# Seven products in place of eight for a second pair of batches, in part of the columns, in a polysketch attention and wave MLP kernel

## The chip, the cores and the metric

One core of a Trainium2 chip runs the whole program. The metric is device time in microseconds, the median of several runs; less is better. The engines work side by side, each through its own list of instructions in order: TensorE (PE; its weight loads are PEld), VectorE (DVE), ScalarE (ACT), GpSimd (POOL) and SyncE (SP, which here only starts transfers).

## What is computed

Four batches of 1088 tokens. An attention with polynomial sketches gives x (128 features a token); x then goes through a mixing step over the tokens. All weights come as float64, and the result is held to float32 accuracy.

```python
def phi(x):                                   # 8 x 8 = 64 features of a head's 32
    a, b = einsum('rd,bhsd->bhsr', S1, x), einsum('rd,bhsd->bhsr', S2, x)
    return einsum('bhsi,bhsj->bhsij', a, b).reshape(..., 64)
kv, z = einsum('bhsf,bhsd->bhfd', phi(k), v), phi(k).sum(2)
x = (phi(q) @ kv) / (phi(q) . z + 1e-06)      # (4, 1088, 4 * 32)
theta = x @ w_theta
y = w_tok_r @ (x * cos(theta)) + w_tok_i @ (x * sin(theta))   # both 1088 x 1088
u = x + y
out = u + relu(u @ w_ch)
```

The costly part is y: for each batch a product of the real and the imaginary token weights, 2 x 1088 x 1088, with z, which is x turned by cos and sin.

## The kernel before

**Lists, not loops.** The program records every operation with its engine and its operands (`Layout.op`), and then issues them in an order written out by hand as numbers (`ORDER`), with the buffer of each temporary given in `PLACES`. Nothing is scheduled at run time: an engine takes its instructions in this order and waits where an operand is not ready or a buffer not free. Nearly all instructions carry the line of a small helper: 312 (matrix product), 292 (VectorE, two tensors), 296 (VectorE, tensor and scalars), 299 (VectorE, `scalar_tensor_tensor`, two tensors and a scalar), 306 (a transfer by POOL that adds to its target). So groups are told apart by their tiles.

**Stages.** For each batch k, q and v are loaded, k is summed into features (`kfeatures`, `key_sums`, `chain`), q is turned and split (`query_slices`), multiplied (`levels`, with the denominator), and `outputs_x` gives x transposed (tile xT, features on partitions, 1152 columns) and from it theta, cos and sin and z. z has 17 chunks of 128 tokens by 128 features: 8 real, 8 imaginary and one of remainders (64 tokens of each). The token weights come as 17 rows w0 to w16 of 128 x 1088, real 0 to 7, imaginary 8 to 15 and 16 the remainders. A row arrives as float64 in a raw buffer (class zs, five in all, which the z of the batches share), ScalarE reads it twice (lines 555 and 557), and VectorE puts it together as float32 (a shift at line 296 and a custom operation at 292).

**Mixing.** For batches 0 and 1, `mix_row` multiplies chunk i of z with row i for all 17 rows into PSUM, in spans of 384, 384 and 320 columns: batch 0 takes all three spans at one row (three PSUM banks), batch 1 a span at a time. These products need only a finished row and the batch's z, and so they fill PE's list while VectorE and ScalarE prepare later batches. `mix_out` adds y to x: for both batches ScalarE copies y out, and POOL adds x by a transfer (`UDMA`). `finish` multiplies with w_ch, applies relu, transposes on VectorE and stores by four transfers from SP.

**The pair 2, 3.** These two batches take one step of Winograd's form of Strassen's scheme. The weights are seen as four quarters: a11 and a12 are the real and imaginary rows in output columns 0 to 543, a21 and a22 in 544 to 1087. With z of batch p (2) and q (3) as the other matrix, seven products of 8 chunks replace eight. They need sums of quarters (`asum`, 8 operations of 544 columns on VectorE each, written over a21 and a12) and differences of z (`zsub`, three operations each). Every product is made in two column parts (`PARTS`: 288 and 256 columns). Products 1 and 2 need neither sums nor differences; 5 needs the first of both, 6 the second, 3, 7 and 4 the later ones. `add` adds each result to xT. So that the differences lose no accuracy, q's z is scaled by a power of two that brings it to p's size: `balance` takes the largest magnitude of x of each batch by two reductions on VectorE, makes the ratio, ScalarE scales x before the turn, and `add` takes the factor out again.

Of the kernel before, what the change touches and what calls it, by code (L numbers as in the profile page):

```python
# [9 lines left out]
F32 = mybir.dt.float32  # L10
# [19 lines left out]
    "6 4 2 5 44 0 1 47 342 3 45 7 50 8 347 49 9 10 11 58 12 29 48 13 76 83 14 46 70 64 15 84 86 16 133 87 77 85 71 "  # L30
    "26 17 139 146 30 89 88 19 72 140 78 73 343 147 74 90 21 18 149 134 27 345 79 91 94 25 150 20 40 80 92 65 32 93 "
    "31 344 41 95 99 127 148 100 43 66 157 151 337 135 22 102 158 101 67 96 128 303 42 68 103 97 348 311 35 28 104 "
    "313 105 36 304 159 305 106 315 160 350 136 108 307 161 306 107 137 109 308 59 23 129 110 314 309 24 111 316 "
    "237 61 112 312 195 33 113 98 130 231 37 238 114 225 115 131 232 152 244 34 69 116 310 233 60 239 226 75 117 "
    "196 123 118 38 81 349 119 120 122 121 346 422 234 357 240 82 424 338 351 53 352 426 425 317 423 153 340 427 "
    "339 428 154 39 429 382 62 124 155 430 141 208 156 125 431 245 201 162 432 126 189 202 197 163 190 433 165 164 "
    "198 318 358 166 191 227 63 434 209 142 359 167 203 435 132 168 436 138 228 367 204 192 169 56 437 171 170 372 "
    "354 438 172 362 143 439 441 173 452 442 174 144 440 353 175 443 51 210 176 445 453 145 444 455 178 446 177 246 "
    "456 179 448 360 447 459 449 180 341 460 461 450 454 181 462 457 182 186 463 183 185 187 184 451 361 521 464 "
    "465 519 355 522 458 466 523 520 356 467 524 468 469 484 525 369 526 527 368 485 470 528 471 377 473 188 57 529 "  # L40
    "472 486 364 530 474 220 531 487 532 363 533 221 374 534 488 392 535 373 542 538 536 549 539 543 537 545 211 "
    "544 550 212 552 546 540 553 247 551 222 215 547 541 213 365 554 548 214 248 475 555 366 556 251 572 558 477 "
    "557 559 574 489 370 560 478 561 575 479 371 564 562 480 476 216 566 563 54 481 252 567 217 249 568 199 569 581 "
    "250 378 483 604 482 605 576 375 570 565 582 218 571 577 606 379 376 573 607 578 387 583 384 579 584 580 253 "
    "393 193 235 223 194 254 224 219 394 255 261 200 265 383 262 608 397 266 205 609 268 267 264 380 585 263 610 "
    "385 206 395 269 323 207 270 389 396 611 586 324 271 321 381 319 587 320 273 588 388 272 274 241 627 322 628 "
    "275 407 390 276 490 412 229 398 831 629 386 277 589 278 399 400 279 630 631 401 402 408 590 612 280 281 632 "
    "297 391 491 835 414 832 492 409 283 410 282 413 411 417 493 403 284 415 291 404 405 494 325 406 495 292 416 "
    "419 496 285 326 286 418 833 327 287 288 290 497 420 293 421 498 289 296 52 834 294 499 500 654 501 507 652 655 "
    "508 650 653 502 298 651 633 256 656 328 634 657 513 332 299 591 658 514 635 659 257 592 660 330 661 636 662 "  # L50
    "593 258 594 55 663 259 331 595 664 333 637 665 596 666 597 673 503 598 329 638 674 334 676 669 335 667 504 639 "
    "677 336 295 505 675 230 300 236 599 668 242 670 680 678 260 243 671 679 681 672 640 688 613 687 683 641 689 "
    "684 695 690 614 691 693 714 692 682 712 694 715 697 716 713 698 301 717 685 699 718 600 686 719 515 720 703 "
    "601 696 705 721 642 700 789 302 701 706 790 516 707 704 702 791 709 780 708 722 615 781 723 616 724 711 808 "
    "517 792 710 518 809 725 617 618 726 619 506 727 810 742 643 620 735 743 728 745 782 744 793 746 838 644 736 "
    "749 621 783 737 738 622 731 729 784 645 730 747 732 739 733 740 734 811 741 798 748 799 750 800 762 751 753 "
    "764 801 765 755 785 752 756 794 766 757 623 768 754 624 758 771 836 812 773 802 759 774 813 770 760 803 761 "
    "795 775 828 763 776 772 767 848 839 777 769 840 841 837 849 778 804 829 850 860 786 851 779 842 886 843 862 "
    "787 852 857 926 830 625 646 788 853 861 796 854 858 868 855 844 856 845 859 864 814 869 797 805 863 877 865 "
    "846 647 878 889 879 870 927 871 887 904 847 880 890 881 930 872 866 806 602 894 867 882 603 883 888 873 928 "  # L60
    "874 967 815 626 807 875 932 905 884 934 509 876 895 892 818 648 896 931 906 933 907 939 929 897 937 940 891 "
    "816 885 941 510 908 935 948 909 936 949 893 898 950 938 924 819 942 910 911 943 951 899 912 952 913 944 925 "
    "953 817 945 820 954 822 821 946 900 649 947 901 968 902 955 903 970 956 957 511 980 958 512 823 971 824 981 "
    "825 982 972 983 826 919 984 920 973 969 974 959 990 961 991 975 921 976 922 923 914 992 960 915 977 916 978 "
    "917 962 979 985 964 963 827 1000 986 918 1001 987 993 965 994 988 1002 966 995 989 996 1004 997 1003 998 1005 "
    "1006 999 1007 1010 1008 1011 1012 1009 1013 1014 "
)
PLACES = (
    "3 1 9 1 1 11 1 21 2 13 15 7 1 9 1 16 6 19 4 0 5 6 0 3 6 3 4 4 1 1 11 3 2 5 6 8 2 1 0 2 4 6 5 2 2 0 7 8 0 1 7 3 "
    "5 5 2 9 6 1 0 4 6 5 7 4 2 1 12 1 7 4 2 0 0 2 0 1 8 4 4 4 3 19 2 5 4 6 14 0 6 0 5 1 7 4 11 1 2 7 8 0 0 7 1 7 21 "  # L70
    "4 0 3 3 7 5 6 1 2 2 6 3 10 12 3 2 2 3 5 8 14 3 4 4 1 4 1 2 2 0 0 6 3 2 2 9 10 5 0 4 0 0 5 21 7 10 7 6 11 3 6 1 "
    "3 0 7 7 11 1 6 4 7 2 6 7 9 5 1 0 4 4 6 7 2 3 7 0 0 2 6 5 3 0 2 3 2 0 12 2 6 8 3 11 10 0 7 18 3 17 5 1 20 17 3 "
    "16 0 4 9 11 3 2 13 2 9 15 3 19 20 1 4 1 1 9 16 1 9 2 3 9 19 2 4 4 3 9 0 7 1 2 11 4 6 0 0 3 5 3 6 0 4 3 4 4 2 2 "
    "5 2 5 6 7 3 3 1 2 7 0 3 6 5 4 3 3 0 2 2 3 5 3 1 0 4 3 2 5 9 7 4 0 4 7 0 2 2 1 2 1 1 3 0 0 7 7 1 3 2 7 2 0 7 7 "
    "4 1 4 1 3 2 3 5 0 0 5 0 1 0 6 3 7 14 6 6 0 3 1 6 5 3 4 3 1 7 1 0 2 4 7 6 1 3 0 6 5 4 5 4 2 0 6 3 4 21 1 21 1 4 "
    "2 5 2 6 2 3 6 4 4 1 1 6 5 0 4 4 3 1 0 0 4 0 6 6 0 1 7 1 4 5 7 14 2 3 0 4 6 2 5 0 2 3 2 6 4 5 4 2 1 6 3 3 2 4 7 "
    "1 5 "
)
SPINS = (
    "76:2 139:4 158:1 109:1 422:1 "  # L80
# [7 lines left out]
PAIR = (2, 3)  # L88
PARTS = ((0, 288), (288, 544))
LAST = (416,)  # L90
APOOL = ()
# [5 lines left out]
UDMA = (True, True, False, False)  # L97
# [128 lines left out]
def kernel(  # L226
# [636 lines left out]
    even = fixed((6,), F32, "even")  # L863
# [122 lines left out]
    def outputs_x(b, lv, pool_qp):  # L986
# [38 lines left out]
        src = xt  # L1025
        if b == PAIR[1]:
            src = balance()
        for g in range(NG):
# [4 lines left out]
            if src is not xt:  # L1033
                xs = buf("g1", (GW,), F32, "xs")
                op("A", act(GW), lambda g=g, xs=xs: A.mul(xs(), xt()[:, g * GW:(g + 1) * GW], even()[:, 4:5]), [xs],
                   cells(xt, g * GW, (g + 1) * GW) + [even])
                off, dep = 0, [xs]
            else:
                xs, off, dep = xt, g * GW, cells(xt, g * GW, (g + 1) * GW)

            def turn(x=x, xs=xs, off=off):
                for i in range(GC):
                    T.transpose(x()[:, i], xs()[:, off + i * P:off + (i + 1) * P], ident())  # L1043

            def theta(g=g, th=th):
# [4 lines left out]
            op("P", 0.67, theta, [th], cells(xt, g * GW, (g + 1) * GW) + [w2])  # L1050
# [11 lines left out]
            vop(2 * full * P, lambda c0=c0, full=full, cs=cs, x=x: tt(  # L1062
                V, z()[:, 0:2 * NF].rearrange("p (t c) d -> p t c d", t=2)[:, :, c0:c0 + full],
                bc(x()[:, 0:full], 1, [P, 2, full, P]), cs()[:, :, 0:full], ALU.mult), [(z, (0, g)), (z, (1, g))],
                [x, cs])
            if full < GC:
                def tail(cs=cs, x=x, full=full):
                    tt(V, z()[0:TL, NK - 1], x()[0:TL, full], cs()[0:TL, 0, full], ALU.mult)
                    tt(V, z()[TL:P, NK - 1], x()[0:TL, full], cs()[0:TL, 1, full], ALU.mult)

                op("V", 0.6, tail, [(z, NG)], [x, cs])

    def balance():
        at("even")
        for j, b in enumerate(PAIR):
            vop(NC * P, lambda j=j, b=b: V.tensor_reduce(out=even()[:, j:j + 1], in_=xT[b](), axis=AX.X, op=ALU.max,
                                                         apply_absolute_value=True), [(even, j)], [xT[b]])

        def ratio():
# [278 lines left out]
```

## Time and profile before

| | us |
|---|---|
| median of 3 runs | 223.38 |
| lowest, highest | 221.67, 223.63 |
| the profiled execution, its own time | 221.87 |
| its span, first to last instruction | 220.1 |

| engine | what it does most | count | busy us | mean ns |
|---|---|---|---|---|
| PE | products of z and w, 384 / 320 / 288 / 256 columns (two records each) | 136 / 68 / 88 / 70 | 50.0 / 23.6 / 26.4 / 19.5 | 489 / 435 / 406 / 381 |
| DVE | rows of w: custom operation, shift | 17, 17 | 21.7, 12.1 | 1284, 718 |
| DVE | sums of w, 544 columns | 32 | 22.3 | 714, 710 |
| DVE | largest magnitudes (line 1076) | 2 | 2.7 | 1348 |
| ACT | rows of w, two reads | 34 | 41.3 | 1216, 1221 |
| ACT | squares with a sum (line 892), and its read | 4, 4 | 4.8, 0.9 | 1194, 226 |
| ACT | scaling of x for batch 3 (line 1035) | 3 | 1.7 | 605 |
| POOL | adding transfers, issue | 12 | 11.5 | 985, 1040 |

Busy time is counted once where records of an engine overlap. On PE records overlap by design, so their mean is longer than the distance between them.

### The profile page before, as it was taken

The numbers are of one execution on the slowest core, as the hardware profiler recorded it, in microseconds if no ns is written. First come the engines' busy times: TensorE is split into PE (matmuls) and PEld (weight loads), VectorE is DVE, ScalarE is ACT, GpSimd is POOL, SyncE is SP. The second block draws the span as 40 slices with busy tenths as digits, with TensorE's granted clock in tenths as the row PEclk, the third lists the DMA queues.
The fourth block names the chain that finished last, engine by engine and source line by source line (L and its number), as shares of the span: only waits on it lengthen the run. The fifth ranks groups of instructions, "written<-read, shape, count | busy, mean of one in ns | idle before, by whom it ended". The sixth has DMA issues, their size and how long they took to land.

```text
span 220.1 us, 5075 instructions
## 1 busy us (share of the span) xinstructions
PE 211.9 (96%) x2045; PEld 160.0 (73%) x2045; DVE 173.8 (79%) x395; ACT 116.8 (53%) x228; POOL 22.7 (10%) x44
## 2 busy tenths in 40 slices
PE   7999996999999999999999999999999999999993
PEld 3787895776678576766667668777688888788872
DVE  4799999999989998988906852899268899955651
ACT  3899989779978986646424455623484000000000
POOL 2465000000050110000222040000200000000000
PEclk9999999999999999999999999999999999999999
DMA  5999189993969763785345342003400002102453
GB/s 177 421 416 390 35 368 356 337 414 102 357 207 255 211 251 133 283 324 206 79 139 91 119 107 42 1 13 56 66 0 0 3 0 47 25 0 43 66 91 75
DMA packets 23195, 34.68 MB, mean 158 GB/s; under 512 B 17028, under 2 KB 18308, under 8 KB 20996
## 3 DMA queue, kind: packets, MB, share of 16 engines
q1 hardware_dynamic: 17908, 29.28, 37.8%
q0 software_dynamic: 1728, 4.65, 9.9%
q10 hardware_dynamic: 3536, 0.43, 1.3%
q8 instruction: 16, 0.26, 0.5%
q14 instruction: 7, 0.06, 0.1%
HBM read 27.48 MB, written 2.23 MB: 135 GB/s over the span
## 4 chain that ended last, share of the span: by engine, by line
PE 83%; DVE 11%; ACT 2%; issue 2%; POOL 1%; POOLq 0%
PE ps L312 74%; PE ps L1010 3%; DVE big L292 3%; DVE g L292 2%; PE ps L1043 2%; PE ps L350 2%; DVE lv L292 1%; PE ps L918 1%; DVE sm L299 1%; DVE hf L296 1%; DVE sm L292 1%; PE ps L694 1%; ACT big L605 1%; ACT g L697 1%; DVE big L296 0%
## 5 line engine op out<-in xcount | busy, mean ns | idle before, releaser
L312 PE MATMUL ps<-big,zs 128*128 128x384 f32 (+4 forms) x398 | 111.6, 423 | 0.4 <-DVE big L292 0.4
L312 PEld LDWEIGHTS ps<-big,zs 128*128 128x128 f32 x398 | 71.2, 190 | 26.7 <-issue 0.8
L1142 ACT COPY g<-ps 128x128 f32<-128x128 f32 (+1 forms) x3 | 0.9, 301 | 48.1 <-PE ps L1134 44.6
L557 ACT ACTIVATE big<-zs 128x1088 int32<-128x1088 uint32 (+1 forms) x18 | 21.1, 1178 | 6.4 <-DMA zs<-w_tok 4.7
L292 DVE CUSTOM_DVE_ANT_0 big<-big,big 128x2176 uint16<-128x2176 uint16 x17 | 21.7, 1284 | 1.5 <-ACT big L557 1.5
L312 PE MATMUL ps<-big,big 128*64 128x64 f32 (+2 forms) x208 | 21.6, 276 | 0.0
L555 ACT ACTIVATE big<-zs 128x1088 f32<-128x1088 f32 x17 | 20.6, 1216 | 0.2 <-DMA zs<-w_tok 0.2
L312 PEld LDWEIGHTS ps<-big,big 128*64 128x64 f32 (+1 forms) x208 | 16.7, 154 | 3.0 <-issue 0.5
L292 DVE TENSOR_TENSOR big<-big,big 128x544 f32<-128x544 f32 x24 | 16.7, 714 | 0.1
L1014 ACT COPY g<-ps 128x384 f32<-128x384 f32 x24 | 10.3, 485 | 11.1 <-PE ps L1010 10.1
L292 DVE TENSOR_TENSOR zs<-ps,g 128x768 f32<-128x768 f32 (+2 forms) x20 | 12.5, 629 | 3.0 <-ACT g L1056 2.6
L306 POOL DMA_DIRECT2D big<-hf x6 | 5.9, 985 | 82.6 <-DVE sm L296 40.7
L296 DVE TENSOR_SCALAR big<-big 128x1088 int32<-128x1088 int32 x17 | 12.1, 718 | 0.1
L292 DVE TENSOR_TENSOR g<-lv 128x768 f32<-128x768 f32 x12 | 11.0, 953 | 0.6 <-PE ps L312 0.5
L312 PEld LDWEIGHTS ps<-w,big 128*128 128x128 f32 x80 | 10.3, 192 | 1.6 <-issue 0.6
L299 DVE SCALAR_TENSOR_TENSOR g<-g,ps 128x384 f32<-128x384 f32 x12 | 6.5, 549 | 5.9 <-ACT g L1052 5.7
L312 PE MATMUL ps<-w,big 128*128 128x128 f32 x80 | 11.1, 277 | 0.0
L1052 ACT ACTIVATE g<-ps 128x384 f32<-128x384 f32 x12 | 5.7, 490 | 7.9 <-PE ps L312 5.3
L1010 PEld LDWEIGHTS ps<-ident,g 128*128 128x128 f32 x72 | 8.2, 141 | 2.3 <-issue 0.8
L1010 PE MATMUL ps<-ident,g 128*128 128x128 f32 x72 | 9.5, 275 | 0.0
L299 DVE SCALAR_TENSOR_TENSOR big<-ps,even,big 128x256 f32<-128x256 f32 (+1 forms) x10 | 4.8, 495 | 5.7 <-PE ps L312 5.7
L312 PE MATMUL ps<-g,sm 128*64 128x384 f32 x48 | 9.1, 499 | 0.0
(185 smaller groups left out, 335.6 us busy)
## 6 DMA issues: line engine op xcount, KB each, us to landing
zs<-w_tok SPq DMA_DIRECT2D x17, 1088.0 KB, 7.0
big<-k_l SPq DMA_DIRECT2D x6, 576.0 KB, 5.9
big<-hf POOLq DMA_DIRECT2D x6, 576.0 KB, 5.6
big<-q_l SPq DMA_DIRECT2D x4, 576.0 KB, 8.7
big<-v_l SPq DMA_DIRECT2D x4, 576.0 KB, 11.0
g<-big POOLq DMA_DIRECT2D x4, 192.0 KB, 3.7
out<-g SPq DMA_DIRECT2D x16, 48.0 KB, 1.8
g<-big POOLq DMA_DIRECT2D x2, 160.0 KB, 3.2
```

The lines of the kernel that those rows point to most:

```text
L292: eng.tensor_tensor(out=o, in0=a, in1=b, op=f)
L296: (eng or V).tensor_scalar(out=o, in0=a, scalar1=s1, scalar2=s2, op0=op0, **kw)
L299: (eng or V).scalar_tensor_tensor(out=o, in0=a, scalar=s, in1=b, op0=op0, op1=op1)
L306: op("G", 0.9, lambda: G.dma_start(dst(), src(), accum_op=ALU.add), w, r, fly=fly)
L312: T.matmul(o, lhs, rhs, start=start, stop=stop, skip_group_check=True)
L350: T.matmul(nowhere(), idle()[:, 0:P], idle(), start=True, stop=True, skip_group_check=True)
L555: op("A", 0.22 + n * 0.0009, lambda: A.activation(dfn(), words_of(raw(), n)[1].bitcast(F32), AF.Prelu, scale=2.0**-112, alpha=-(2.0**32)), ...
L557: op("A", 0.22 + n * 0.0009, lambda: A.activation(stp(), words_of(raw(), n)[0].bitcast(U32), AF.Copy, scale=2.0**-29), [stp], [raw])
L1010: T.transpose(tr()[:, i * P:(i + 1) * P], qp()[:, i * H + 2 * n:i * H + 2 * n + 2].rearrange("p h i j -> p (h i j)"), ident())
L1014: op("A", act(GW), lambda n=n, tr=tr, qT=qT: A.copy(qT()[:, n], tr()), [(qT, n)], [tr])
L1043: T.transpose(x()[:, i], xs()[:, off + i * P:off + (i + 1) * P], ident())
L1052: op("A", act(GW), lambda cs=cs, th=th: A.activation(cs()[:, 0], th(), AF.Copy, bias=ROUND), [(cs, 0)], [th])
```

## The change

Batches 0 and 1 become a second pair (`PAIRS`). In the second column part (256 of each 544 columns, `FEW = 1`), their products are those of the seven-product scheme as well; in the first part (288 of each half) they stay direct, now in spans of 288. Since the sums of w are written over the quarters, both pairs take each step before the next sum: `winograds` goes through the steps, and at each first makes the sum and then the products of pair 0, 1 and of pair 2, 3. The differences of z for the first pair go to one buffer of class zs, for the second pair partly to smaller buffers (`spare`). For the pair 0, 1, product 5 is added to both quarters of batch 1 by VectorE, and product 3 has a bank of its own, where the pair 2, 3 goes on adding in PSUM.

The scales now come from the sum of magnitudes of all of x: ScalarE makes it for each batch with its accumulator (`AF.Abs`, the elements go to the still unused z), a product with ones adds over the partitions, and VectorE makes the ratio, once for each pair. The factor is no longer applied by ScalarE to x; the multiply that makes z takes it as a scalar operand (`scalar_tensor_tensor` in place of `tensor_tensor`) for batches 1 and 3. Batch 1's direct part takes it out on VectorE in `mix_out`, and POOL's adding transfers remain for batch 0 alone (two, of 288 columns). `ORDER`, `PLACES` and `SPINS` (idle products that keep PE running early on) are new throughout.

```diff
-PAIR = (2, 3)
+PAIRS = ((0, 1), (2, 3))
+FEW = 1
-UDMA = (True, True, False, False)
+UDMA = (True, False, False, False)
...
+        op("A", act(NC * P) + 0.12, lambda: A.activation(z()...[:, 0:NC * P], xt(), AF.Abs,
+                                                         accum_out=even()[:, b % 2:b % 2 + 1]), [z, (even, b % 2)], [xt])
+        if b % 2:
+            balance(PAIRS[b // 2], even)
+        def times(dst, x, c):
+            if b % 2:
+                stt(dst, x, even()[0:x.shape[0], 4:5], c, ALU.mult, ALU.mult)
+            else:
+                tt(V, dst, x, c, ALU.mult)
...
-                op("A", act(GW), lambda g=g, xs=xs: A.mul(xs(), xt()[...], even()[:, 4:5]), [xs], ...)
...
-            vop(NC * P, lambda j=j, b=b: V.tensor_reduce(out=even()[:, j:j + 1], in_=xT[b](), axis=AX.X, op=ALU.max,
-                                                         apply_absolute_value=True), [(even, j)], [xT[b]])
+        op("P", 0.1, lambda: mm(tot(), ones(), even()[:, 0:2], True, True), [tot], [even])
...
+        def one():
+            product("5", by, t1, a21, [(q, 1)] if p else [(q, 1), (q, 0)])
+            zsub("2", t2, im_q, t1)
...
+            product("3", by if p else each("pw"), im_q, a12, [(q, 0)], (q, 0), fresh=not p)
...
+    def winograds():
+        both = [winograd(PAIRS[0], (FEW,), (), lambda: two_in("zs")),
+                winograd(PAIRS[1], range(len(PARTS)), LAST, lambda: (spare("t1", ...), spare("t2", ...)))]
+        sums = [("1", a21, a21, a22, ALU.add), ("2", a21, a21, a11, ALU.subtract), ("4", a12, a12, a21, ALU.subtract),
+                ("3", a21, a22, a21, ALU.subtract)]
+        for k, s_ in enumerate([None] + sums):
+            if s_:
+                asum(*s_)
+            for steps in both:
+                steps[k]()
...
-        cuts = tuple(range(0, S, GW))
+        if b < 2:
+            spans = [(h * len(PARTS) + j, h * HT + c0, h * HT + c1) for h in range(2)
+                     for j, (c0, c1) in enumerate(PARTS) if j != FEW]
```

## The prediction

> **What bounds the kernel now.** First the page's shares, its 40 slices and the windows of 10 us.
>
> ```profile
> PE 211.9 (96%) x2045; PEld 160.0 (73%) x2045; DVE 173.8 (79%) x395; ACT 116.8 (53%) x228; POOL 22.7 (10%) x44
> ...
> DVE  4799999999989998988906852899268899955651
> ...
> PEclk9999999999999999999999999999999999999999
> ```
>
> ```profile
> 50.00:60.00 10.00, 10.00 (x40) 6.51 (x39) 9.68 (x18) 9.67 (x12) 0.00 (x0) 1.00 0.61 216
> ...
> 100.00:110.00 10.00, 10.00 (x34) 6.27 (x33) 9.90 (x23) 5.17 (x5) 1.30 (x1) 1.00 0.49 153
> 110.00:120.00 10.00, 10.00 (x124) 7.28 (x122) 2.79 (x7) 4.10 (x8) 2.60 (x3) 1.00 0.49 117
> ```
>
> After the size of a window stand PE's, PEld's, DVE's, ACT's and POOL's busy time. From 40 us on PE is never short of work, at full clock. But up to 110 us VectorE is full too; only then has it gaps. So there are two regimes: before 110 us both engines are full, after it PE alone. Next the timeline, VectorE's and then PE's, where these meet:
>
> ```profile
> 34.17 1.35 DVE L292 TENSOR_TENSOR big<-big,hf 128x1152 f32<-128x1152 f32 x1
> 35.44 0.45 DVE L967 TENSOR_REDUCE sm<-lv 128x36 f32<-128x288 f32 x1
> ...
> 107.93 1.29 DVE L292 CUSTOM_DVE_ANT_0 big<-big,big 128x2176 uint16<-128x2176 uint16 x1
> ```
>
> ```profile
> 92.43 21.43 PE L312 MATMUL ps<-big,zs 128*128 128x320 f32 x70
> 113.79 0.57 PE L312 MATMUL ps<-mv,hf 128*64 128x96 f16 x18
> ...
> 216.15 0.39 PE L312 MATMUL ps<-w,big 128*128 128x128 f32 x2
> ```
>
> The operation at 107.93 finishes row 16, the last row of w, at 109.2. PE multiplies it just ahead of 113.79, at about 111.95 (its 1088 columns take 1.84). So PE was 2.7 us behind VectorE there: it had other products to do, and VectorE's rows were no limit. Two prices follow. The 70 records are 35 products, 30 of batch 0 (10 rows of 1088 columns) and 5 of batch 1, 12,608 columns in 21.36 us: 1.69 ns a column. On VectorE an operation of n elements lasts n/960 + 0.15 us, and the next starts 0.085 before its end (34.17 + 1.35 against 35.44).
>
> **PE's work.** Batches 0 and 1 now cost 2 x 17 x 1088 = 36,992 columns. After: 17 rows x 576 columns x 2 = 19,584, seven products of 8 x 256 = 14,336, and four remainder rows of 256 = 1,024: 34,944. That is 2,048 columns, 3.5 us less. Two products with ones (the row of such has 248 ns) and 26 more, narrower products take back about 0.5. PE's list is **3.0 us shorter**.
>
> **Where the removed columns stood.** I added up PE's list in program order, for both kernels, up to the first product that reads row 16. Everything but w products is the same there: 55.5 us. Of w products 44.8 us stand ahead of that point before, and 31.4 after: the direct products need only a row and z, and 47% of their columns are gone; of the seven products that replace them, five wait for sums of w or of z, which come after the last row in VectorE's list. So 13.4 us of cover moves behind the point. Behind it stood 103.3 us by price, and it took 216.54 - 111.95 = 104.6. After, 10.3 more stand there (13.4 less the 3.0): **114.9**.
>
> **VectorE's list up to row 16.** It was busy 99.9 of the first 109.2 us (the windows' sums) and idle 9.4: 5.5 before 60 us, mostly at the start, and 3.9 from there on, waiting for ScalarE, rows and PE. What the change moves behind the point is four sums of w (0.714 long, 0.63 back to back): -2.5. What it puts ahead of it is nearly nothing: one scale (five tiny operations, 0.85), against fewer of the small steps of the chain, and a scalar pointer in five multiplies. That operation is not in the trace with such operands; the nearest rows are 511 ns with pointer against 456 without (288 elements), so 0 to 0.06 each; I take 0.05, 0.25 in all. Left: 97.6. The 5.5 idle stay. Of the 3.9, waits on PE vanish (PE's products that VectorE needs stand 8 us and more earlier in the lists than their use, where they stood 1.3 apart before), those on rows can stay: 0 to 3.9, and I take 0.6, since ScalarE's list up to the last row grows too. So row 16 is ready at **103.7**, 5.5 us earlier than now, while PE's list alone would be there 13.4 earlier. PE now passes the point at 111.95 with 100.3 us of work done, 11.7 of waits; then at 103.7 with 86.9, 16.8 of waits: some **5 us new**, against 3.0 of work saved.
>
> **Added on ScalarE.** Four sums of magnitudes with accumulation, by the row of the squares 1.19 + 0.23 = 1.4 each, 5.7; three scalings of 605 ns and four copies (1.8 + 2.0) go: +1.9. Two of the four stand ahead of row 16, between copies for PE. ScalarE idles 0.3 to 1.8 a window there, so I put them at nothing; without that cover it is 1.4 each on rows and copies alike, 2.8.
>
> **VectorE later.** Two reductions go (1.348 each). It gains twelve differences of z (0.55, 0.55, 0.42 four times: 6.1), nine additions of 256 columns (three at 0.408, six at 0.478: 4.1), two finishes of batch 1 (1.0), some 0.7 in the other finishes and the second scale: +10 us by these rows, on 73 busy of 110 us behind the point. It fits, but VectorE takes its list in order, and each of the four sums of w (8 x 0.63 = 5.1) must now wait until both pairs have read the old quarter; PE's next product waits behind it. Those places had slack before and after by the lists, of 0.1 to 0.5 us at six of them after. 0 to 2.4; I take 0.
>
> **Queues.** POOL loses four of its twelve additions in flight (about 1 us of issue each, 3.2 to 3.7 to land). SP issues 32 stores for batches 0 and 1 in place of 24, 0.5 each, and one group of four now stands just ahead of the two that end the program. They need 2.0 us and are ready some 2.5 earlier; 0 to 0.5, taken at 0. The end after PE's last product stays 3.6 (220.1 - 216.54).
>
> **The sum.** 103.7 + 114.9 + 3.6 = **222.2 of span**, against 220.1: +2.1, 1.0%. (From VectorE's end to PE's start it is under 0.1: the chain of waits has 215.65 + 0.30 and then 215.99.) Before, by the same sum, 109.2 + 104.6 + 3.6 = 217.4, under the 220.1 that PE's list set: this chain had 2.7 us of slack and now has none. The profiled execution took 221.87, 1.8 over its span and 0.7% under the median of 223.38, so I scale the median: 223.38 x 222.2/220.1 = **225.5**. With the ends of the unknown costs (0 and 3.9 of waits, -0.25 for the pointer; late sums and stores are rival 3): 221.4 to 225.5 of span, 224.7 to 228.9.
>
> [...]
>
> **Rivals.**
> 1. The gain arrives. Row 16 must be ready by 98.6 for the whole of it (220.1 - 3.0 = 217.1 of span, 220.3). For: the first loads are reordered, and some of the 5.5 us of early idle may go. Against: 97.6 of VectorE work leaves 1.0 for all of its waits. Row 16 at 101 would make 219.5, 222.8, no change.
> 2. Slower by more: the rows come late. A row took 5.05 and 5.2 us from issue to ScalarE's read (issues at 88.15 and 99.53, reads at 93.20 and 104.74), and three buffers carry them while five are shared with z. The last may be issued once row 12 has been read. If that is later than 95.0, then 5.2 + 2.3 + 1.2 sets row 16 and not VectorE. Were all rows as late as now, less the 2.5 of moved sums: 106.7, span 225.2, time 228.6. For: ScalarE waited 4.7 us for rows. Against: transfer engines are half idle then.
> 3. The late sums cost: PE waits 0.4 at each of six tight places, 2.4 more: span 224.6, time 227.9; with the stores' 0.5, 228.4. For: VectorE's order is fixed and now serves two pairs. Against: it idles a third of that stage.
> [...]
>
> That the change does not do what it says I rule out: the lists show seven products and the four sums.
>
> **Numbers.** Forecast 0.50; rival 1: 0.16, 2: 0.17, 3: 0.14, 4: 0.03. About 1% (221.1 to 225.6 here) is what this kernel's runs can tell from no change: they lie between 221.67 and 223.63. The forecast stands on the upper bound, so half of it, 0.25, is within 1%, and of rival 1 the partial cases, 0.05: same 0.30. Faster is the rest of rival 1, 0.11; slower 0.25 + 0.17 + 0.14 + 0.03 = 0.59. The range takes in the forecast's bounds and rivals 2 to 4 as priced; it leaves out the faster part of rival 1, 0.11, and the worst of 2, 0.05: 221.2 to 228.9.
>
> **What would show it.** Right: PE's busy share falls, with some 5 us of new waits on VectorE between 35 and 105 us; row 16 finished near 103.7; some 115 us of full PE behind it. Wrong: row 16 ready before 100, or PE waiting below 1 us a window there (rival 1); the last row's read waiting for its transfer (2); PE waiting between 140 and 200 us (3); a granted clock below 1.00 (4).

## The result, and the profile after

| | before | after |
|---|---|---|
| time, median of 20 runs each (us) | 222.32 (221.23 to 223.63) | 224.54 (223.06 to 226.59) |
| ratio, 95% interval | | 1.0103 (1.0081 to 1.0124) |
| profiled execution: time, span (us) | 221.87, 220.1 | 225.0, 223.2 |
| its mean granted clock of PE | 1.000 | 0.977 |

Slower by 1.0%; the forecast was 0.95% (225.5 on 223.38) and 222.2 us of span. On the median that the forecast started from, the ratio makes 225.7. The profiled execution is not the usual one of the changed kernel: of its 20 runs two have a clock of 0.975 to 0.977, one has 1.000 (224.06 us, 222.1 of span), and the others have 0.985 to 0.992. The page of the changed kernel, its shares and two rows of the 40 slices:

```profile
PE 214.3 (96%) x2101; PEld 173.2 (78%) x2101; DVE 180.4 (81%) x425; ACT 118.1 (53%) x229; POOL 21.6 (10%) x40
...
DVE  4898999978999999999999679726999957434642
...
PEclk9988999589999999999999999999999999999999
```

VectorE is now busy 90% or more from the 11th slice to the 22nd (56 to 123 us), and the clock is no longer full: it falls twice. PE's busy share is 96% as before, and its busy time has even risen by 2.4 us though its list is shorter, for 10.2 us of it passed at half clock (last section). In after_light, an experiment below without half clock, it is 213.0, idle products of 1.1 included. The windows that answer to those of before, and one more:

```profile
40.00:50.00 10.00, 10.00 (x124) 7.93 (x126) 8.53 (x20) 7.60 (x16) 0.00 (x0) 0.70 0.79 321
50.00:60.00 10.00, 9.63 (x90) 7.46 (x85) 8.75 (x25) 9.77 (x20) 0.00 (x0) 1.00 0.36 103
...
100.00:110.00 10.00, 10.00 (x125) 8.03 (x124) 9.86 (x25) 5.69 (x9) 0.86 (x1) 1.00 0.52 134
110.00:120.00 10.00, 10.00 (x64) 8.22 (x65) 9.50 (x26) 1.91 (x7) 1.15 (x2) 1.00 0.27 75
```

The timeline, VectorE's last row of w and then PE's places around it:

```profile
102.78 1.29 DVE L296 CUSTOM_DVE_ANT_0 big<-big,big 128x2176 uint16<-128x2176 uint16 x1
```

```profile
54.29 1.13 PE L316 MATMUL ps<-big,zs 128*128 128x256 f32 x4 [0.25 <-DVE zs L296]
...
96.47 8.89 PE L316 MATMUL ps<-big,zs 128*128 128x256 f32 x36
...
219.60 0.39 PE L316 MATMUL ps<-w,big 128*128 128x128 f32 x2
```

Row 16 is finished at 104.07 (forecast 103.7). Its first product is the last pair but one of the 36 records and starts at 104.21, 0.1 later (before: 2.7 later). From there to PE's last product it takes 115.8 (forecast 114.9), from there to the end 3.2 (forecast 3.6).

So the sum came out. But PE did not wait for row 16 itself. What last held it ahead of that row was a step of the chain, a product with ones that takes a reduction from VectorE:

```profile
95.95 0.22 DVE L808 TENSOR_REDUCE sm<-ps 128x8 f32<-128x64 f32 x1
```

```profile
96.23 0.39 PE L316 MATMUL ps<-sm,ones 128*128 128x8 f32 x2
```

From that product PE takes 7.98 us to the first pair of row 16, by price with 0.1 us of pauses in all. It takes as long in the profiles of all nine variants of the changed kernel below as well, and the pair starts 0.14 or 0.15 us after row 16 is ready, be that at 101.0 or at 105.9. So VectorE does set PE's date there, but at this step, 8 us ahead of the row that the prediction named.

Nor did the waits come where they were put. Here are the windows of the stretch from PE's first product for z to row 16, before (50.3 to 111.9) and after (54.3 to 104.2):

```profile
50.30:111.90 61.60, 61.48 (x446) 41.15 (x445) 55.67 (x109) 44.36 (x68) 5.76 (x6) 1.00 0.67 220
```

```profile
54.30:104.20 49.90, 48.99 (x430) 38.30 (x431) 49.31 (x93) 42.56 (x66) 7.08 (x6) 1.00 0.76 251
```

After the change both engines are full there: PE idles 0.9 us, VectorE 0.6. Before, VectorE had 5.9 us to spare.

To see where PE loses time I went through its operations one by one: the distance from one's start to the next one's, less the price of its kind (the 20th percentile of that distance over all operations of the kind in fourteen profiles). Besides the two kernels the table has two experiments from below, each the same kernel with idle products inside PE's waits; their clocks are 1.000 and 0.999, so they are the cleaner pair. PE's first operation starts at 1.3 us; the first two rows and these 1.3 make the third.

| us | before | after | before_light | after_light |
|---|---|---|---|---|
| list up to the first product for z, by price | 40.9 | 40.5 | 42.2 | 41.6 |
| above price up to there | 8.0 | 12.5 | 6.3 | 9.0 |
| PE's first product for z starts | 50.3 | 54.3 | 49.9 | 52.0 |
| list from there to the end, by price | 161.4 | 158.1 | 161.4 | 158.1 |
| above price, each 0.03 to 0.2 (number) | 3.4 (38) | 4.8 (54) | 3.4 (38) | 4.9 (55) |
| above price, each over 0.2 (number) | 1.0 (3) | 2.2 (5) | 1.0 (3) | 3.6 (6) |

PE's list became 3.7 us shorter, as meant (0.4 and 3.3). What ate it: 4.5 us more lost ahead of the first product for z, 1.4 in hand-offs (places where PE starts about 0.1 us later than back to back, after another engine's work), and 1.2 in new waits; PE's last product starts 3.45 us later, and the shorter end leaves 3.1 of span.

### The profile page after: what moved, and what is told of

The parts are those of the page before. It is cut to its first block, busy times and chain, and to the rows that moved or that the text cites. A ratio compares the mean times of both kernels' runs of the same rounds, so it can differ in the third digit from the quotient of the medians.

```text
span 223.2 us, 5223 instructions
## 1 busy us (share of the span) xinstructions
PE 214.3 (96%) x2101; PEld 173.2 (78%) x2101; DVE 180.4 (81%) x425; ACT 118.1 (53%) x229; POOL 21.6 (10%) x40
## 3 DMA queue, kind: packets, MB, share of 16 engines
q0 software_dynamic: 1152, 3.83, 7.3%
## 4 chain that ended last, share of the span: by engine, by line
PE 82%; DVE 7%; DMA 5%; ACT 3%; issue 1%; POOL 0%; SPq 0%; DVEq 0%
PE ps L316 72%; PE ps L1014 5%; DMA big<-hf 3%; PE ps L922 3%; DMA big<-k_l 2%; DVE big L296 1%; PE ps L1053 1%; DVE lv L296 1%; ACT big L609 1%; ACT big L896 1%; DVE g L296 1%; ACT g L701 1%; DVE big L303 1%; PE ps L698 1%; POOL big L310 0%
## 5 line engine op out<-in xcount | busy, mean ns | idle before, releaser
L316 PE MATMUL ps<-big,zs 128*128 128x288 f32 (+2 forms) x450 | 110.0, 388 | 0.6 <-DVE big L296 0.4
L316 PEld LDWEIGHTS ps<-big,zs 128*128 128x128 f32 x450 | 80.1, 190 | 18.0 <-issue 1.5
L303 DVE SCALAR_TENSOR_TENSOR big<-ps,even,big 128x256 f32<-128x256 f32 (+1 forms) x16 | 7.5, 482 | 17.0 <-PE ps L316 17.0
L316 PE MATMUL ps<-big,big 128*64 128x64 f32 (+2 forms) x176 | 13.9, 255 | 1.0 <-DMA big<-hf 0.7
L310 POOL DMA_DIRECT2D big<-hf x6 | 6.5, 1089 | 71.0 <-ACT g L1018 40.9
L1014 PEld LDWEIGHTS ps<-ident,g 128*128 128x128 f32 x72 | 9.5, 159 | 4.5 <-ACT big L714 1.7
L1014 PE MATMUL ps<-ident,g 128*128 128x128 f32 x72 | 11.6, 307 | 1.2 <-DVE sm L300 1.1
L316 PEld LDWEIGHTS ps<-big,big 128*64 128x64 f32 (+1 forms) x176 | 10.7, 147 | 2.6 <-issue 0.9
L316 PEld LDWEIGHTS <-hf 128*64 128x64 f16 (+1 forms) x288 | 8.0, 113 | 1.4 <-issue 0.9
L296 DVE TENSOR_TENSOR zs<-ps,g 128x768 f32<-128x768 f32 (+2 forms) x10 | 6.3, 630 | 3.1 <-ACT g L1066 2.9
L316 PE MATMUL ps<-big,g 128*128 128x288 f32 (+1 forms) x32 | 8.6, 396 | 0.0
```

Source lines behind the costliest of these rows:

```text
L296: eng.tensor_tensor(out=o, in0=a, in1=b, op=f)
L303: (eng or V).scalar_tensor_tensor(out=o, in0=a, scalar=s, in1=b, op0=op0, op1=op1)
L310: op("G", 0.9, lambda: G.dma_start(dst(), src(), accum_op=ALU.add), w, r, fly=fly)
L316: T.matmul(o, lhs, rhs, start=start, stop=stop, skip_group_check=True)
L1014: T.transpose(tr()[:, i * P:(i + 1) * P], qp()[:, i * H + 2 * n:i * H + 2 * n + 2].rearrange("p h i j -> p (h i j)"), ident())
```

## The experiments

All ratios are to the kernel before, measured beside each; 1.0103 is the changed kernel's own.

**Is it VectorE's list up to row 16, or PE and its clock?** Four more shifts on VectorE, in the changed kernel and in the one before:

```diff
         def shift():
             ts(dfn().bitcast(I32), dfn().bitcast(I32), 3, ALU.logical_shift_left)
+            if stage in ("row6", "row7", "row8", "row9"):
+                ts(dfn().bitcast(I32), dfn().bitcast(I32), 0, ALU.logical_shift_left)
```

> The changed kernel with the shift of rows 6 to 9 of w followed by a shift by zero bits on VectorE: four more operations of 1088 elements, 0.63 us back to back, 2.5 us ahead of row 16, the output unchanged. Theory A (VectorE's list up to row 16 sets the end): row 16 at 106.5 instead of 104.05, 2.5 us on the time, a ratio of 1.021 to 1.022 to the kernel before. Theory B (PE's own pace sets the end: the stretches in which its clock is halved, 3.3 us near 16 and 6.6 us from 39.5, and its longer list behind): VectorE has room, 0 to 0.5 us, a ratio of 1.010 to 1.013.

Measured: 226.66 us, 1.0205 (1.0157 to 1.0254): 2.1 us more. Row 16 at 105.87, 1.8 later (2.6 later if counted from the first z, which in this execution came 0.8 earlier), and PE follows 0.15 after it. PE's longest wait is for row 5 of w:

```profile
70.61 0.70 PE L317 MATMUL ps<-big,zs 128*128 128x256 f32 x2 [1.68 <-DVE big L297]
```

VectorE has no room in the changed kernel: A upwards.

> The kernel before with the same four shifts by zero bits, 2.5 us more of VectorE ahead of row 16. By the prediction its PE came to row 16 2.7 us after VectorE had it, so VectorE has room for them: A gives a ratio of 1.000 to 1.003. If VectorE's list set the end of the kernel before as well, 2.5 us and 1.011.

Measured: 224.37, 1.0102 (1.0051 to 1.0153), against the 0 that I expected. In its profile the span is 1.3 us longer: PE waits 0.61, 0.36 and 0.35 us at 73.3, 75.5 and 93.4, for z and for a step of the chain (the product with ones that is named above), though it still comes to row 16 3.4 us after VectorE (113.11 against 109.76). A part of the 1.0% is the clock. The three runs at 0.996 or more have a median of 223.14, those of the kernel before at such a clock 221.64; the three others (0.989 to 0.992) have 225.22 against 223.42. That leaves 1.5 to 1.8 us for the 2.5 that were added. So of the 2.7 us at the last row at most 1 was slack of the chain: it is tight at places ahead of it.

Then the other way, eight shifts fewer:

```diff
         def shift():
-            ts(dfn().bitcast(I32), dfn().bitcast(I32), 3, ALU.logical_shift_left)
+            if stage not in tuple(f"row{i}" for i in range(3, 11)):
+                ts(dfn().bitcast(I32), dfn().bitcast(I32), 3, ALU.logical_shift_left)
```

> The changed kernel without the shift of rows 3 to 10 of w (their products are of other numbers): eight operations of 0.63, 5.0 us of VectorE ahead of row 16. A: row 16 at 99.0, and the span falls by 5.0 from 223.2 to 218.2, as long as PE's own list (217.1 by the prediction) allows it: a ratio of 0.985 to 0.992 to the kernel before. B: no more than 0.5 us, a ratio of 1.008 to 1.010.

Measured: 223.99, 1.0073 (1.0040 to 1.0107). Row 16 is ready only 2.4 earlier, since VectorE now waits itself, longest for a product and ScalarE's copy of it:

```profile
67.84 1.48 DVE L304 SCALAR_TENSOR_TENSOR g<-g,ps 128x384 f32<-128x384 f32 x3 [2.06 <-ACT g L1068]
...
100.38 1.29 DVE L297 CUSTOM_DVE_ANT_0 big<-big,big 128x2176 uint16<-128x2176 uint16 x1
```

Of the 2.4 us, 1.0 is lost again behind row 16, where PE waits 0.7 for an addition of POOL at 107.87. A falls in this direction: 5 us less of VectorE are worth 0.3%.

**The clock.** Idle products are put ahead of an operation into its own PSUM bank, which its real product then overwrites:

```diff
+MORE = "158:1 139:1 307:1 132:3 174:3 441:6"   # operation: idle products ahead of it
...
+                    if b.cls == "ps":
+                        for _ in range(more.pop(o.i, 0)):
+                            fill(raw)
```

> The changed kernel with 15 more idle products of 384 columns on PE, ahead of six operations near 14 us and between 34 and 40 us, twelve of them ahead of PE's three longest waits there (0.51, 0.42, 1.09 us); each is 0.16 us at full clock, 2.4 in all, some 1.4 of it inside waits. They are to keep the clock from being halved near 16 and from 39.5 to 46.1 us. A, strictly: clock 1.00, but VectorE's date for row 16 stays at 104, and the time too: a ratio of 1.009 to 1.012. B: PE gains 1.6 and 3.3 us, VectorE's waits of 1.15 and 1.26 near 46 and 50 us go, row 16 is ready at 101.7, and the span is some 221: a ratio of 1.000 to 1.003.

Measured: 225.11, 1.0131 (1.0090 to 1.0171), at clocks of 0.996 to 1.000. Half clock was not what made it slower. But here 2.4 us of idle products were added (15 of 0.16: in the trace of before one takes 0.33 us at 32.59, two take 0.49 at 7.80), not all inside waits. So later only seven, inside two waits (`MORE = "174:2 441:5"`):

> The changed kernel with seven idle products, two inside PE's wait of 0.42 us at 38.0 and five inside the wait of 1.09 us at 38.8: nothing is put in where PE has work. If they keep the clock from being halved from 39.5 on, and that half clock is what the first z waits for: first w product at 51 instead of 54.3 us, time 222 to 223. If VectorE and the additions in flight take its place, as with 15 such products: 224 to 225, at a clock of 0.99 to 1.00.

Measured: 224.37, 1.0090 (1.0056 to 1.0125), clock 0.996 to 0.999. The first product for z comes 2.3 us earlier than in the changed kernel's profile, and yet the median is only 0.2 us lower. The timeline of PE, with the idle products first, and the chain of waits around 70 us:

```profile
39.02 0.97 PE L360 MATMUL ps<-idle 128*128 128x384 bf16 x5 [0.24 <-ACT sm L739]
...
51.96 1.13 PE L322 MATMUL ps<-big,zs 128*128 128x256 f32 x4 [0.25 <-DVE zs L302]
...
73.18 1.27 PE L322 MATMUL ps<-big,big 128*64 128x64 f32 x36 [1.24 <-DMA big<-hf]
...
108.42 0.72 PE L322 MATMUL ps<-g,w 128*128 128x288 f32 x2 [0.68 <-DMA g<-big]
```

```profile
64.56 1.09 POOL big L316
65.64 0.21 issue
65.86 7.18 DMA big<-hf
73.04 0.14 issue
73.18 4.75 PE ps L322 x62
```

An adding transfer that POOL issued at 64.56 takes 7.18 us (median of its kind on the page: 5.2), and PE waits for it. Against the changed kernel's profile 0.6 of the 2.3 us go again at 73.18 and 0.8 at 108.42; the span is 0.9 shorter. With PE earlier here, it is POOL's additions that it waits for (1.24 and 0.68). The same handful in the kernel before (`MORE = "166:3 172:5"`):

> The kernel before with eight idle products, three inside PE's wait of 0.66 us at 33.7 and five inside the one of 1.05 us at 37.3. Of its 41 runs 27 had a clock of 0.998 to 1.000 and 219.3 to 220.5 us of span, 12 one of 0.991 to 0.992 and mostly 221.2 to 221.8. If the idle products keep the clock up: all runs near 221.5, a ratio of 0.994 to 0.999. If they only add to PE's list: 222 to 223 and 1.000 to 1.006.

Measured: 221.40, 0.9950 (0.9923 to 0.9976), all twelve runs between 221.03 and 222.16, clock 0.997 to 1.000. **This version beats both kernels.** What it gains is the clock: the 41 runs of the kernel before at 0.997 or more have a median of 221.59 as well. The five idle products stand where PE waited 1.05 us:

```profile
37.72 0.99 PE L356 MATMUL ps<-idle 128*128 128x384 bf16 x5
```

**Is PE's list worth anything ahead of row 16?** Six of eight terms of one product are left out, once of a product at 54.8 to 87.8 us and once of one at 185 to 194 us (`THIN` names the product's stage):

```diff
-                            mm(ps()[:, o:o + w], ...)
+                            if stage != THIN or i in (0, NF - 1):
+                                mm(ps()[:, o:o + w], ...)
```

> The changed kernel without six of the eight terms of one of the seven products (rows 1 to 6 of batch 0's first product in the second column part, which stand between 54.8 and 87.8 us): 6 x 0.44 = 2.6 us less of PE ahead of row 16. Theory A (up to row 16 PE is paced by others, VectorE first, so that its own list is worth nothing there): 0 to -0.5 us, 224.0 to 224.5. Theory B (PE's list and its clock set the end from the start): -2.6, 221.9.

> The same six terms left out of a product that stands at 185 to 194 us, behind row 16: 2.6 us less of PE where it has no waits in the profile. A and B alike: -2.6 us, 221.9. If VectorE, which also finishes the output there, sets the end: less than 1 us.

Measured: ahead 224.12, 1.0097 (1.0062 to 1.0131), next to nothing; behind 223.26, 1.0026 (0.9989 to 1.0063), 0.8% less, where 2.6 us would be 1.2%. In the profile of the second (220.37, the fastest of its runs) the stretch from row 16 to PE's last product is 113.4 against 115.8, 2.4 shorter: behind row 16 PE's list counts nearly in full. In the profile of the first, waits of PE take the place of the products: among them 0.67 and 0.42 for operands from VectorE at 59.4 and 61.8, 0.42 and 0.83 for POOL's additions at 71.7 and 74.1. The same on the kernel before, with row 1 and a third of row 2 left out for batch 0 (`b, i, t0` are batch, row and first column):

```diff
             for (g, t0, t1), yp in zip(gs, yps):
+                if (b, i, t0) in ((0, 1, 0), (0, 1, 384), (0, 1, 768), (0, 2, 0)):
+                    continue
                 mm(yp()[:, :t1 - t0], z()[:, i], rows[i]()[:, t0:t1], i == 0, i == NK - 1)
```

> The kernel before without the product of row 1 for batch 0 and the first third of row 2 (1472 columns, 2.5 us of PE at 50 to 55 us). By the prediction PE came to row 16 2.7 us after VectorE: the 2.5 us arrive, 219.4 to 219.8, a ratio of 0.989. Theory D's counterpart (VectorE already paced the kernel before at places ahead of row 16, as the 2.4 us that four more shifts cost there suggest): 0 to -0.8, a ratio of 0.996 to 1.000.

Measured: 221.85 in the nine runs at a clock of 0.985 or more (222.47 in all twelve), 0.9989 (0.9954 to 1.0025). The five at 1.000 have 221.08, the kernel before at full clock 221.59: 0.5 of the 2.5 us arrive. PE comes to row 3's product early and waits there for the next part of z:

```profile
49.44 3.18 PE L313 MATMUL ps<-big,zs 128*128 128x384 f32 x10
54.55 2.10 PE L313 MATMUL ps<-big,zs 128*128 128x384 f32 x6 [1.93 <-DVE zs L293]
```

So the kernel before was not bound by PE's list alone from 40 us on, as the prediction had it. PE was hardly ever idle, but it had less than half a microsecond in hand at that z, which PE uses at 55.74 there and VectorE has ready at 55.3:

```profile
54.35 0.96 DVE L292 TENSOR_TENSOR zs<-ps,g 128x768 f32<-128x768 f32 x1
```

**ScalarE's sums.** Each sum of magnitudes over 64 of 1152 columns, alone and with the eight shifts left out:

```diff
-        A.activation(z().rearrange("p c d -> p (c d)")[:, 0:NC * P], xt(), AF.Abs, ...)
+        A.activation(z().rearrange("p c d -> p (c d)")[:, 0:64], xt()[:, 0:64], AF.Abs, ...)
```

> The changed kernel with each sum of magnitudes on ScalarE made over the first 64 of 1152 columns only: four operations of 1.22 us become some 0.35, and the first of each pair no longer waits for all three groups of columns of its batch before z may be written. The prediction put these sums at nothing: by it 0 to -0.3 us. Theory C (the sum stands on the path to the first z of batch 0, which VectorE had at 48.5 us before and at 54.2 now): the first z is ready 1 to 1.5 us earlier, and the time falls by 1 to 1.5, to 223.0 to 223.5.

> Both reliefs at once: the short sums on ScalarE, and no shift of rows 3 to 10 of w on VectorE (5.0 us). The latter alone gave 223.99. If VectorE and ScalarE together are what PE waits for, the gain now arrives: 221 to 222. If neither is, it stays at 223.5 to 224: then PE's list, its clock, or the additions in flight that POOL issues hold the rest.

Measured: 224.43, 1.0089 (1.0048 to 1.0131), and 223.42, 1.0078 (1.0051 to 1.0105). The sums are worth nothing that can be measured, as the prediction put them; theory C falls. And VectorE and ScalarE relieved by 5 and 3.5 us together still leave it slower than before.

**VectorE and PE relieved together** (the edits of after_minus and after_ahead in one kernel):

> The changed kernel without the shift of rows 3 to 10 (VectorE 5.0 us less) and without the six terms of batch 0's first product (PE 2.6 us less ahead of row 16). Alone they gave 223.99 and 224.12 against 224.54, 0.55 and 0.4. Theory D (from the first z on PE and VectorE are both full and equally long, so that either alone is worth little): together 2 to 2.6 us, 222.0 to 222.5. If neither holds the kernel there (something earlier or the additions in flight do), no more than the sum of the two: 223.5 to 224.

Measured: 223.21, 1.0045 (1.0015 to 1.0075), 0.6% less than the changed kernel, some 1.3 us: more than either alone, less than D asked for. Not settled by it.

**What all of these have in common** is the first product for z. In every profile of the changed kernel and its variants (z ready between 51.2 and 54.2) it starts within 0.1 us of the end of VectorE's operation that makes the first part of z, after a wait of about 0.25 or more. From the end of that operation to row 16 it takes 49.8 us in the changed kernel and 49.1 to 51.3 in its variants, also with eight shifts fewer, six of them behind that z (49.4), or with six terms fewer (50.0); only the four added shifts make it 52.4. So the date of row 16 follows that of the first z. Before, that z was ready at 48.5 and PE came to it at 50.3, without a wait:

```profile
50.26 5.97 PE L312 MATMUL ps<-big,zs 128*128 128x384 f32 x19
```

VectorE's timeline from the step ahead of it (44.74 before, 46.79 after) to that z (47.58, 53.29), first before, then after:

```profile
44.74 0.54 DVE L299 SCALAR_TENSOR_TENSOR g<-g,ps 128x384 f32<-128x384 f32 x1
...
45.75 1.28 DVE L292 CUSTOM_DVE_ANT_0 big<-big,big 128x2176 uint16<-128x2176 uint16 x1
46.95 0.72 DVE L296 TENSOR_SCALAR big<-big 128x1088 int32<-128x1088 int32 x1
47.58 0.95 DVE L292 TENSOR_TENSOR zs<-ps,g 128x768 f32<-128x768 f32 x1
```

```profile
46.79 0.56 DVE L303 SCALAR_TENSOR_TENSOR g<-g,ps 128x384 f32<-128x384 f32 x1 [1.15 <-ACT g L1062]
47.26 2.49 DVE L296 CUSTOM_DVE_ANT_0 big<-big,big 128x2176 uint16<-128x2176 uint16 x2
51.01 0.46 DVE L300 TENSOR_SCALAR big<-lv 128x576 f32<-128x576 f32 x1 [1.26 <-ACT lv L957]
51.50 0.76 DVE L296 TENSOR_TENSOR lv<-lv,big 128x576 f32<-128x576 f32 x1
...
52.62 0.75 DVE L303 SCALAR_TENSOR_TENSOR big<-lv 128x576 f32<-128x576 f32 x1
53.29 0.95 DVE L296 TENSOR_TENSOR zs<-ps,g 128x768 f32<-128x768 f32 x1
```

In the new order two rows of w and three larger steps stand between the two; before, one operation and one shift of rows, the rest steps of 0.2 us. From the one to the other it is 2.8 us before and 6.5 after, and still 5.4 (45.60 to 50.96) in after_light, where no half clock adds waits. That explains why the shorter sums on ScalarE brought nothing: the z that waits for them has its turn on VectorE only later (at 51.19 in that profile, with the short sums). A version with this z earlier in VectorE's list was not tried, so its worth stays open.

## Why the prediction was right, and where it was not

- **PE's list 3.0 us shorter:** right, 3.7 by prices (0.4 ahead of the first product for z, 3.3 from there).
- **Row 16 at 103.7:** right, 104.07. The parts were each off by 2 us and cancelled: VectorE was busy 95.9 of it, not 97.6, and idle 8.2, not 6.1. That they cancelled is luck; with the clock kept up (after_light) the row is ready at 102.29. 2.4 of the idle time are the two waits of 1.15 and 1.26 near 46 and 50 us, during and behind PE's half-clocked stretch, which are neither in the kernel before nor in after_light. And what holds PE is a reduction 8 us ahead of the row, not the row.
- **114.9 behind it, 3.6 at the end:** right, 115.8 and 3.2. Where PE also waits for POOL's addition near 108 us, as in after_light, the stretch is 116.7.
- **"some 5 us new waits" of PE on VectorE between 35 and 105 us:** the size was roughly right (PE lost 7.1 us more in the whole span, of which 1.4 are hand-offs), the place was not. Of it 4.5 lie ahead of the first product for z at 54.3, in this execution largely as 10.2 us at half clock (with the clock kept up, 9.0 us above price instead of 12.5); between there and row 16 PE is 98% busy. The sign that was named for rival 1, waits below 1 us a window, was there without its gain, and the sign that was named for the forecast, a lower busy share of PE, was not there (96% before and after).
- **"this chain had 2.7 us of slack and now has none":** the step that failed. Two experiments show that the kernel before had no such slack: 2.5 us more of VectorE cost 1.0% (1.5 to 1.8 us at equal clock), 2.5 us less of PE brought 0.1% (0.5 us at full clock). The 2.7 us were read at one place, the last row; z (0.4 us in hand at row 3) and the chain were tighter.
- **ScalarE's sums at nothing:** right (1.0089 against 1.0103 with them cut short); one takes 1.3 with its read (51.93 to 53.24), not 1.4, for the read starts ahead of its end. The pointer operand costs 0.06 in the multiply that makes z, the upper bound: 1.01 against 0.95 at 768 columns.
- **Rival 1** did not come. **Rival 2:** not the rows (VectorE's longest wait between 60 us and row 16 is 0.20), but other transfers were late: POOL's additions, which I had only counted as fewer (0.68 at 74.95 in this profile, over 1 us where PE is earlier). **Rival 3** fell: from 120 us on PE loses 2.6 us above price in the changed kernel and 1.9 before, with no new wait among them. **Rival 4**, whose sign was a clock below 1.00: the clock did fall, twice, but without one long gap (the longest wait was 1.09 us), and with the clock kept up the median falls by no more than 0.2 us; in the kernel before the price is 1.8 us (last section). No run shows the price that the range and the chance of 0.03 take for it; what the runs showed is 3.4 or 6.8 us at half clock.
- **VectorE's price, n/960 + 0.15 us:** in the trace of before it holds for operations of two tensors (1.35 at 1152 elements, 0.95 at 768, 0.71 at 544), but not for the shift (0.72 at 1088).

So the forecast's number rests on a sum that held at its ends; the reason it gave for the loss in between, VectorE's row dates alone, is a part of it. The sum also took full clock for both kernels. At full clock the span is 219.8 us before, and 222.1 in the changed kernel's one such run and 222.4 in after_light: 2.3 to 2.6 more, where 2.1 was forecast. Shown is that VectorE, PE's list and the clock, each relieved alone, give back at most 0.3% ahead of row 16. What all the relief together would reach stays open.

## What to carry to other kernels

Slack read at one meeting point of two engines is not the slack of the stage: look for the tightest point ahead of it, and test by adding work, not only by taking it away. Work saved on the engine that is always busy was worth little where others hand it its operands just in time (0.4 of 2.6 us in after_ahead); see which stretch is left when it is moved. Idle products inside waits kept the clock up here (0.997 to 1.000 in before_light, whose median is 221.40, where the kernel before has 223.40 at 0.991 or 0.992).

## What the runs showed of the hardware

The clock of PE fell without a long wait. Windows of 1 us of the changed kernel:

```profile
38.00:39.00 1.00, 0.37 (x3) 0.30 (x2) 1.00 (x5) 1.00 (x7) 0.00 (x0) 1.00 1.00 418
39.00:40.00 1.00, 0.12 (x1) 0.15 (x2) 0.96 (x4) 1.00 (x2) 0.00 (x0) 0.62 1.02 417
40.00:41.00 1.00, 1.00 (x6) 1.00 (x7) 1.00 (x4) 0.40 (x2) 0.00 (x0) 0.50 1.01 409
...
46.00:47.00 1.00, 1.00 (x9) 0.63 (x9) 0.21 (x1) 0.74 (x2) 0.00 (x0) 0.97 1.11 445
```

From the clock shares, half clock began at 39.24 (0.62 is 0.76 us of half clock) and ended at 46.06: 6.8 us. An earlier stretch lasted from 15.3 to 18.8, 3.4 us. In the 3.4 us ahead of the later one PE had waited 0.87 us (0.42, and 0.45 of the wait of 1.09), in those ahead of the earlier one 0.29 us (0.23, and 0.06 of a wait of 0.15). The variants after_minus and after_plus have one stretch each up to 47.5 us, from 38.94 to 42.36 and from 41.23 to 44.64: 3.4 us again, half as long as the stretch of 6.8. The variant after_spin, with its idle products, has the clock at 1.00 up to 47.5. A long wait was not behind it: once PE had started, none in the changed kernel's profile was longer than 1.09, and before_ahead, with one of 1.93 us at 52.6 to 54.55, has a mean clock of 1.000. What made the clock fall, perhaps the small products that stand there, was not separated.

By their mean clock, some runs of the kernel before have the same: beside the experiments 41 of its runs had a clock of 0.997 or more and 219.3 to 220.6 us of span, 28 one of 0.991 or 0.992 and 220.2 to 221.9. As an estimate from these means, 0.008 of some 220 us is 1.8 us of PE's work, and half clock of 3.4 us takes 1.7. There it shows in the time, with medians of 221.59 and 223.40; it was most of the spread of 221.2 to 223.6. In the changed kernel the same loss is one of several that overlap: its runs at 0.988 lie from 223.06 to 225.94, on both sides of the one at 1.000, and the idle products moved the median by 0.2 us.
